# An attention loop with its negation and sums ahead of the copies, and the first weight loads later

## Chip, cores and metric
The kernel runs on one core of a Trainium2 chip. The metric is the device time of one execution in microseconds (us), the median of several runs. The engines work side by side, each through its own instructions in order, and wait for each other by semaphores: TensorE (PE; its weight loads PEld), VectorE (DVE), ScalarE (ACT), GpSimd (POOL), and SyncE (SP), which here only issues DMA transfers.

## What is computed
Attention over a sliding window of 64, then a mixture of experts with one expert a token, then a gated feed-forward layer:

```python
# q, k, v: (4, 8, 576, 64), window 64
scores = np.where(mask, scale * np.matmul(q, k.transpose(0, 1, 3, 2)), -1000000000.0)
attn = np.exp(scores - np.max(scores, axis=-1, keepdims=True))
attn = attn / (np.sum(attn, axis=-1, keepdims=True) + 1e-09)
x = np.matmul(attn, v)                    # as (2304, 512)
# each token goes to one of 8 experts of 288 places: h = relu(x @ w1[e]) @ w2[e]   (512 -> 1024 -> 512)
g = x @ w_gate; val = x @ w_val           # 512 -> 1536
out = (g / (1 + np.exp(-g)) * val) @ w_out
```

## The kernel before
**Stages.** Attention with the logits of the routing fills the first 123 us, the routing itself goes on to about 165 us, and the rest are the experts and the gated layer, which run on PE almost without a gap. The order of every engine's instructions is that in which the Python code emits them.

**Attention.** There are 16 pairs of batch and head pair, each with 9 blocks of 64 queries. Four such blocks make a group, so there are 36 groups (`NG`), and the loop of line 344 has a step `i` for each. Its steps overlap several groups:

- in even steps `scores(i // 2)`: PE writes the masked scores of two groups, `i` and `i + 1`, into two of three banks `ps_s`;
- `maxima(i)` (DVE, L216): the rows' maxima, from `ps_s` to `nm`; `negated(i)` (DVE, L219) multiplies `nm` in place by the negative scale;
- `exponents(i - 1)` (ACT, L226): four activations with `nm` as bias, to `pp`, with the rows' sums in `sm`;
- `transposed(i - 3)`: PE (L241) turns the normalised tile `pn` into a bank `ps_t`, and ACT copies it to `pt` (L249);
- in odd steps `values((i - 5) // 2)` (PE, L256), in even ones `out_x` (DVE, L272) copies its result to `xT` (in the rows `big`); a few steps also have a product for the logits (L280) with its copy (L285);
- `take(i)`: preparation of later queries and keys, mostly one q and one k a step: PE transposes them (L184) into two banks `ps_t`, then DVE (L190), or ACT (L188) for the second half of a k, copies them to `qt` and `kt`. In odd steps it also has POOL copy values, `vw` (L172);
- `norms(i - 1)`: DVE adds a tiny number to the sums (L231) and takes the reciprocal (L232), and POOL multiplies `pp` by it, giving `pn` (L236).

The banks `ps_t` are three in a ring for `pn` transposes and preparations together. `load(h)` issues the DMAs of a head pair's q, k (L163) and v (L167) on SP, three to five pairs ahead. Each waits until its buffer is free, and SP issues in order.

**First weights.** After step 27 (`3 * NC`) the loop emits `convert_move()`, three transfers `raw` (L869) for the gated layer, and `st.load(4)`, four transfers `wraw` (L43) for the experts, 512 KB each. `wraw` is first read in the routing, by ACT (L59, `whi<-wraw`).

Of the kernel before, what the change touches and what calls it, by code (L numbers as in the profile page):

```python
# [68 lines left out]
class Kernel:  # L69
# [30 lines left out]
    def attention(self, ctx):  # L100
        nc = self.nc
        B, H, S, D = self.q.shape
        HP, NC = H // 2, S // 64
# [47 lines left out]
        NG = len(units) // 4  # L151
# [23 lines left out]
        def prep(name, b, hp, x):  # L175

            if name == "v":
                copy_v(b, hp, x)
                return
            if not x:  # L180
                tr[name, b, hp] = kt_p.tile([128, S], F32, name=name + "t")
            ps = ps_t.tile([128, 3, 96], F32, name="ps_t")
            for t in range(3):
                nc.tensor.transpose(ps[:, t, :], raw[name, b, hp][:, 3 * x + t].rearrange("p s d -> p (s d)"),  # L184
                                    self.ident[0:96, 0:96])
            dst = tr[name, b, hp][:, 288 * x:288 * x + 288].rearrange("p (t i) -> p t i", t=3)
            if name == "k" and x:
                nc.scalar.activation(dst, ps, AF.Copy)  # L188
            else:
                nc.vector.tensor_copy(dst, ps)  # L190
# [3 lines left out]
        def scores(G):  # L194

            us = units[8 * G:8 * G + 8]
            for h in range(2):
                SS[2 * G + h] = ps_s.tile([128, 4, 128], F32, name="ps_s")
            for r in range(2):
                first = ([4 - m for m in range(4) if us[2 * m + r][1] == 0] or [0])[0]  # L200
                for h, sl in enumerate(sides):
                    mm(SS[2 * G + h][sides[r]], identb[sl, sl], mask[sl, first:first + 4], start=True, stop=False)
            for m in range(4):
                for r in range(2):
                    b, c, hp = us[2 * m + r]
                    for h, sl in enumerate(sides):
                        k = tr["k", b, hp][sl]
                        kk = k[:, 64 * c - 64:64 * c + 64] if c else k[:, None, 0:64].to_broadcast([64, 2, 64])
                        mm(SS[2 * G + h][sides[r], m, :], tr["q", b, hp][sl, 64 * c:64 * c + 64], kk,
                           start=False, stop=m == 3)  # L210
# [3 lines left out]
        def maxima(g):  # L214
            NM[g] = small.tile([128, 4], F32, name="nm")
            nc.vector.tensor_reduce(NM[g], SS[g], axis=AX.X, op=OP.max)  # L216

        def negated(g):
            nc.vector.tensor_scalar(NM[g], NM[g], -scale, None, op0=OP.mult)  # L219

        def exponents(g):
            ps, nm = SS[g], NM[g]
            PP[g] = work.tile([128, 4, 128], F32, name="pp", bufs=2)
            SM[g] = small.tile([128, 4], F32, name="sm")
            for u in range(4):
                nc.scalar.activation(PP[g][:, u, :], ps[:, u, :], AF.Exp, bias=nm[:, u:u + 1], scale=scale,  # L226
                                     accum_out=SM[g][:, u:u + 1])

        def norms(g, halves=False):
            sm = SM[g]  # L230
            nc.vector.tensor_scalar(sm, sm, 1e-9, None, op0=OP.add)  # L231
            nc.vector.reciprocal(sm, sm)  # L232
            PN[g] = work.tile([128, 4, 128], F32, name="pn", bufs=4)
            for eng, u in ((nc.gpsimd, slice(0, 1)), (nc.vector, slice(1, 4))) if halves else ((nc.gpsimd, slice(0, 4)),):
                n = u.stop - u.start
                eng.tensor_tensor(PN[g][:, u], PP[g][:, u], sm[:, u, None].to_broadcast([128, n, 128]), op=OP.mult)  # L236

        def transposed(g, late=False):
            ps = ps_t.tile([128, 4, 128], F32, name="ps_t")
            for u in range(4):  # L240
                nc.tensor.transpose(ps[:, u, :], PN[g][:, u, :], self.ident)  # L241
            PT[g] = work.tile([128, 4, 128], F32, name="pt", bufs=3)
            if late == 2:
                nc.vector.tensor_copy(PT[g][:, 0:2], ps[:, 0:2])
                nc.scalar.activation(PT[g][:, 2:4], ps[:, 2:4], AF.Copy)
            elif late:
                nc.vector.tensor_copy(PT[g], ps)
            else:
                nc.scalar.activation(PT[g], ps, AF.Copy)  # L249

        def values(G, j0=0, n=8, p=ps_o, name="ps_o"):
            ps = OO[G, j0] = p.tile([128, n, 64], F32, name=name)
            for j in range(j0, j0 + n):
                b, c, hp = units[8 * G + j]
                for h, sl in enumerate(sides):
                    mm(ps[sl, j - j0, :], vw(b, hp)[:, c, h, :], PT[2 * G + h][:, j // 2, sides[j % 2]],  # L256
                       start=True, stop=True)
# [19 lines left out]
        def logits(t0, n, ps_p=ps_o, name="ps_o", act=False):  # L277
            ps = ps_p.tile([128, n], F32, name=name)
            for hp in range(HP):
                mm(ps[32 * hp:32 * hp + 32, :], wgp[:, hp, :], xT[:, hp, t0:t0 + n], start=True, stop=True)  # L280
            LT[t0] = work.tile([128, n], F32, name="lt", bufs=2)
            if act:
                nc.scalar.activation(LT[t0], ps, AF.Copy)
            else:
                nc.vector.tensor_copy(LT[t0], ps)  # L285

        def logits2(t0, n, ps_p=ps_o, name="ps_o"):
            lt = LT[t0]
            k = n // 128
            pl = ps_p.tile([128, k, 128], F32, name=name)  # L290
            for i in range(k):
                nc.tensor.transpose(pl[:, i, :], lt[:, 128 * i:128 * i + 128], self.ident)
            nc.vector.tensor_reduce(self.L[:, t0 // 128:t0 // 128 + k, :],
                                    pl.rearrange("p k (a e) -> p k e a", a=HP)[:, :, 0:NE, :], axis=AX.X, op=OP.add)
# [3 lines left out]
        def load(h):  # L298

            if h < NP:  # L300
                load_rows("q", h // HP, h % HP)
                load_rows("k", h // HP, h % HP)
            if 0 < h <= NP:
                load_v((h - 1) // HP, (h - 1) % HP)
# [13 lines left out]
        for h in reversed(range(NP)):  # L318
            for a in (("k", 1), ("q", 1), ("k", 0), ("q", 0)):

                i = 2 * ((h * NC + 4 * a[1]) // 8) - (1 if h < 2 else 2)
# [10 lines left out]
        for h in range(NR, NP + 1):  # L332

            i = max(ready[h - NR] if h < NP else 0, 2 * (((h - NV) * NC - 1) // 8) + 6 if h > NV else 0)
            loads.setdefault(i + 1, []).append(h)

        def take(i):
            for h, (name, x) in todo.get(i, ()):
                prep(name, h // HP, h % HP, x)
# [4 lines left out]
        for i in range(NG - 1):  # L344
            for h in loads.get(i, ()):
                load(h)
            if i % 2 == 0:
                scores(i // 2)
            maxima(i)
            if i >= 1:  # L350
                exponents(i - 1)
            if i >= 3:
                transposed(i - 3)
            if i % 2 and i >= 5:
                values((i - 5) // 2)
            if late:
                logits2(*late)
                if late[0] + late[1] == 128 * self.n0:
                    window = self.first_window(ps_o.tile([128, 1], F32, name="ps_o"))
                late = None  # L360
            if i % 2 == 0 and i >= 6:
                if done < 1536 and S * (8 * (i - 6) // 2 // (HP * NC)) >= done + 512:
                    late = (done, 512)
                    logits(*late)
                    done += 512
                out_x((i - 6) // 2)
            take(i)
            negated(i)
            if i >= 1:
                norms(i - 1)  # L370
            if i < NC or i % 2:
                next(made, None)
            next(window, None)
            if i == 3 * NC:
                self.convert_move()
                self.st.load(4)

# [772 lines left out]
```

## Time and profile before
| | us |
|---|---|
| median of 3 runs | 837.43 (835.99 to 837.7) |
| profiled execution | 837.32 |
| its span, first to last instruction | 835.5 |

| engine | busy us | share of the span |
|---|---|---|
| PE | 788.7 | 94% |
| PEld | 732.2 | 88% |
| DVE | 514.8 | 62% |
| ACT | 373.9 | 45% |
| POOL | 125.6 | 15% |

A busy share over the whole span mixes the stages. The stage that a change lies in is read by itself, by the busy time in stretches of it and by what ended each wait there. The granted clock of PE stands in tenths of its full 2.4 GHz; 0.5 is its lower level, 1.2 GHz. A busy time of a small instruction includes time in which it was held up after its start.

### The profile page before, as it was taken

How to read it: one execution, taken by the hardware profiler on the slowest of the kernel's cores; microseconds unless marked ns; L12 is line 12 of the kernel's file. 1: busy time of each engine (PE TensorE's matmuls, PEld its weight loads, DVE VectorE, ACT ScalarE, POOL GpSimd, SP SyncE). 2: the span in 40 equal slices, each digit the busy share in tenths (PEclk: the TensorE clock that was granted, in tenths of full speed). 3: DMA queues.
4: the chain of work that ended last, by engine and by line, in shares of the span. 5: the costliest groups of instructions: out<-in, count | busy, mean ns of one | idle time of the engine just before them, and what ended most of it. 6: DMA issues, size and time to landing. Idle time of an engine off the chain costs nothing.

```text
span 835.5 us, 15332 instructions
## 1 busy us (share of the span) xinstructions
PE 788.7 (94%) x5895; PEld 732.2 (88%) x5895; DVE 514.8 (62%) x1078; ACT 373.9 (45%) x947; POOL 125.6 (15%) x206
## 2 busy tenths in 40 slices
PE   7889786499999999999999999999999999999997
PEld 5767665399999999999999999999999999999996
DVE  5787678678888888898774443544453455344322
ACT  3877646346665666575332333323232243222211
POOL 6767643400010000000000000210000011000002
PEclk8999998699999999999999999999999999999999
DMA  9866706669898897777632211331211223220001
GB/s 183 175 149 138 221 2 213 196 200 286 276 288 271 276 287 263 243 258 263 204 118 69 77 51 50 114 114 51 76 52 51 75 89 114 76 68 10 1 1 76
DMA packets 109742, 119.57 MB, mean 143 GB/s; under 512 B 61280, under 2 KB 77664, under 8 KB 109664
## 3 DMA queue, kind: packets, MB, share of 16 engines
q1 hardware_dynamic: 106784, 109.09, 43.2%
q0 software_dynamic: 2880, 9.44, 3.3%
q8 instruction: 49, 0.80, 0.4%
q14 instruction: 29, 0.24, 0.1%
HBM read 99.63 MB, written 18.87 MB: 142 GB/s over the span
## 4 chain that ended last, share of the span: by engine, by line
PE 43%; issue 33%; DVE 2%; POOL 2%; DMA 0%; ACT 0%; POOLq 0%; DVEq 0%; ACTq 0%
PE psw L937 12%; PE psg L937 12%; PE psa L937 11%; PE pso L937 6%; POOL out_dram L1082 1%; PE psw L969 1%; DMA w<-t 0%; DVE wlo L60 0%; PE psw L431 0%; DVE sg L1054 0%; DVE t L890 0%; DVE t L894 0%; ACT xt L929 0%; DVE y L930 0%; POOLq L1146 0%
## 5 line engine op out<-in xcount | busy, mean ns | idle before, releaser
L937 PE MATMUL psg<-y,whi 128*128 128x384 f32 x1152 | 223.1, 336 | 0.0
L937 PEld LDWEIGHTS psg<-y,whi 128*128 128x128 f32 x1152 | 201.6, 188 | 0.0
L60 DVE TENSOR_TENSOR wlo<-wraw,whi 128x512 fp32r<-128x512 f32 x236 | 155.3, 687 | 8.8 <-ACT whi L59 4.3
L59 ACT ACTIVATE whi<-wraw 128x512 fp32r<-128x512 f32 x236 | 136.6, 622 | 2.8 <-ACTq L668 2.8
L1050 DVE TENSOR_TENSOR sg<-sg,psg 128x384 f32<-128x384 f32 x72 | 39.8, 553 | 156.1 <-ACT sg L1049 156.0
L937 PE MATMUL pso<-whi,p 128*128 128x512 f32 x432 | 133.3, 390 | 0.0
L937 PE MATMUL psg<-y,wlo 128*128 128x384 f32 x576 | 123.5, 336 | 0.7 <-DVE sg L1050 0.7
L1049 ACT ACTIVATE sg<-psg 128x384 f32<-128x384 f32 x72 | 35.3, 491 | 174.6 <-PE psg L937 174.6
L937 PEld LDWEIGHTS psg<-y,wlo 128*128 128x128 f32 x576 | 102.5, 188 | 3.8 <-DVE sg L1050 1.2
L937 PEld LDWEIGHTS pso<-whi,p 128*128 128x128 f32 x432 | 80.6, 188 | 14.5
L1056 ACT ACTIVATE p<-sg 128x384 fp32r<-128x384 f32 x72 | 37.8, 525 | 120.7 <-DVE sg L1054 120.7
L1082 POOL DMA_INDIRECT out_dram<-orow,idx x18 | 17.5, 971 | 456.9 <-ACT orow L1080 270.9
L937 PE MATMUL pso<-wlo,p 128*128 128x512 f32 x216 | 84.2, 390 | 0.0
L937 PE MATMUL psw<-xt,whi 128*128 128x288 f32 x512 | 78.5, 296 | 0.0
L937 PE MATMUL psa<-hl,whi 128*128 128x288 f32 x256 | 75.6, 295 | 0.1
L937 PE MATMUL psa<-hh,whi 128*128 128x288 f32 x256 | 75.5, 295 | 0.0
L937 PE MATMUL psa<-hh,wlo 128*128 128x288 f32 x256 | 75.3, 294 | 0.0
L937 PEld LDWEIGHTS psw<-xt,whi 128*128 128x128 f32 x512 | 71.5, 188 | 0.0
L1057 DVE TENSOR_TENSOR p<-sg,p 128x384 fp32r<-128x384 f32 x72 | 40.2, 558 | 42.6 <-ACT p L1056 42.6
L226 ACT ACTIVATE pp<-ps_s,nm 128x128 f32<-128x128 f32 x144 | 51.0, 372 | 25.9 <-DVE sm L231 22.7
L1054 DVE TENSOR_TENSOR sg<-sg,psg 128x384 f32<-128x384 f32 x72 | 39.8, 553 | 21.0 <-PE psg L937 21.0
L926 ACT ACTIVATE hh<-psw 128x288 fp32r<-128x288 f32 x64 | 26.3, 411 | 58.3 <-PE psw L937 58.3
(177 smaller groups left out, 1063.6 us busy)
## 6 DMA issues: line engine op xcount, KB each, us to landing
wraw<-in_moe_w_dram SPq DMA_DIRECT2D x64, 512.0 KB, 5.1
wraw<-w SPq DMA_DIRECT2D x54, 512.0 KB, 3.3
w<-t SPq DMA_DIRECT2D x36, 256.0 KB, 3.6
raw<-in_moe_w_gate_dram SPq DMA_DIRECT2D x12, 512.0 KB, 5.2
raw<-in_moe_w_val_dram SPq DMA_DIRECT2D x12, 512.0 KB, 5.9
raw<-in_moe_w_out_dram SPq DMA_DIRECT2D x12, 512.0 KB, 5.3
rawq<-in_q_dram SPq DMA_DIRECT2D x32, 144.0 KB, 3.4
rawk<-in_k_dram SPq DMA_DIRECT2D x32, 144.0 KB, 3.9
```

The costliest lines, as they stand in the source:

```text
L59: self.nc.scalar.activation(h[sl], t[sl], AF.Copy)
L60: self.nc.vector.tensor_tensor(lo[sl], t[sl], h[sl].bitcast(F32), op=OP.subtract)
L226: nc.scalar.activation(PP[g][:, u, :], ps[:, u, :], AF.Exp, bias=nm[:, u:u + 1], scale=scale, accum_out=SM[g][:, u:u + 1])
L926: nc.scalar.activation(h, x, AF.Relu)
L937: self.nc.tensor.matmul(acc, x, y, start=start and i == 0, stop=stop and i == len(seq) - 1)
L969: nc.tensor.transpose(ps[:, d, :], self.xg[t][r0:r1, 128 * d:128 * d + 128], self.ident[r0:r1, r0:r1])
L1049: nc.scalar.activation(sg, pg, AF.Sigmoid)
L1050: nc.vector.tensor_tensor(sg, sg, pg, op=OP.mult)
L1054: nc.vector.tensor_tensor(sg, sg, pv, op=OP.mult)
L1056: nc.scalar.activation(p[0][:, sl], sg, AF.Copy)
L1057: nc.vector.tensor_tensor(p[1][:, sl], sg, p[0][:, sl].bitcast(F32), op=OP.subtract)
L1082: d = nc.gpsimd.indirect_dma_start(out=self.out, out_offset=bass.IndirectOffsetOnAxis(ap=self.idx[:, 6 * g + t:6 * g + t + 1], axis=0), in ...
```

## The change
`negated(i)` moves from the end of the step to just behind `maxima(i)`. `take(i)` moves behind `norms(i - 1)`. The first weight loads are emitted after step 32 (`NG - 4`, 36 groups) instead of step 27.

```diff
@@ -347,6 +347,7 @@
             if i % 2 == 0:
                 scores(i // 2)
             maxima(i)
+            negated(i)
             if i >= 1:
                 exponents(i - 1)
             if i >= 3:
@@ -364,14 +365,13 @@
                     logits(*late)
                     done += 512
                 out_x((i - 6) // 2)
-            take(i)
-            negated(i)
             if i >= 1:
                 norms(i - 1)
+            take(i)
             if i < NC or i % 2:
                 next(made, None)
             next(window, None)
-            if i == 3 * NC:
+            if i == NG - 4:
                 self.convert_move()
                 self.st.load(4)
```

On DVE, in the middle of the loop, an even step (with `out_x`) and the odd step behind it, before:

```order
L216 TENSOR_REDUCE nm<-ps_s 128x4
L272 COPY big<-ps_o 128x256 x2
L190 COPY qt<-ps_t 128x288
L219 TENSOR_SCALAR nm<-nm 128x4
L231 TENSOR_SCALAR sm<-sm 128x4
L232 RECIPROCAL sm<-sm 128x4
L216 TENSOR_REDUCE nm<-ps_s 128x4
L190 COPY qt<-ps_t 128x288
L190 COPY kt<-ps_t 128x288
L219 TENSOR_SCALAR nm<-nm 128x4
L231 TENSOR_SCALAR sm<-sm 128x4
L232 RECIPROCAL sm<-sm 128x4
```

And after, the same two steps:

```order
L216 TENSOR_REDUCE nm<-ps_s 128x4
L219 TENSOR_SCALAR nm<-nm 128x4
L272 COPY big<-ps_o 128x256 x2
L231 TENSOR_SCALAR sm<-sm 128x4
L232 RECIPROCAL sm<-sm 128x4
L190 COPY qt<-ps_t 128x288
L216 TENSOR_REDUCE nm<-ps_s 128x4
L219 TENSOR_SCALAR nm<-nm 128x4
L231 TENSOR_SCALAR sm<-sm 128x4
L232 RECIPROCAL sm<-sm 128x4
L190 COPY qt<-ps_t 128x288
L190 COPY kt<-ps_t 128x288
```

The negation stands right behind the maxima of its group, the output copies lie between it and the sums, and the copies of q and k end the step.

On POOL, early in the loop (`-` before, `+` after; `below` and `base` are constants of the routing):

```order
 L525 MEMSET below_395 128x18
 L525 MEMSET below_396 128x18
+L236 TENSOR_TENSOR pn<-pp,sm 128x512
 L172 TENSOR_TENSOR vw_141<-vw_141,vone 64x384 x2
 L172 TENSOR_TENSOR vw_141<-vw_141,vone 64x256
-L236 TENSOR_TENSOR pn<-pp,sm 128x512
```

The value copies of an odd step go behind that step's `pn`. All through the loop two `pn` still lie between two groups of value copies, but it is another of the two that follows them.

On SP, at the end of the attention's loads (`rawq`, `rawk`, `vw` are the last two head pairs' rows, `xrows` the row stores after attention):

```order
 L163 DMA rawk<-in_k_dram 96x6x64 x2
 L167 DMA vw_143<-in_v_dram 64x9x64 x2
-L869 DMA raw_1785<-in_moe_w_gate_dram 128x2x512
-L869 DMA raw_1787<-in_moe_w_gate_dram 128x2x512
-L869 DMA raw_1789<-in_moe_w_val_dram 128x2x512
-L43 DMA wraw<-in_moe_w_dram 128x4x256
-L43 DMA wraw<-in_moe_w_dram 128x2x512
-L43 DMA wraw<-in_moe_w_dram 128x4x256
-L43 DMA wraw<-in_moe_w_dram 128x2x512
 L163 DMA rawq<-in_q_dram 96x6x64 x2
 L163 DMA rawk<-in_k_dram 96x6x64 x2
 L167 DMA vw_144<-in_v_dram 64x9x64 x2
```

and directly below these rows:

```order
 L167 DMA vw_140<-in_v_dram 64x9x64 x2
+L869 DMA raw_2056<-in_moe_w_gate_dram 128x2x512
+L869 DMA raw_2058<-in_moe_w_gate_dram 128x2x512
+L869 DMA raw_2060<-in_moe_w_val_dram 128x2x512
+L43 DMA wraw<-in_moe_w_dram 128x4x256
+L43 DMA wraw<-in_moe_w_dram 128x2x512
+L43 DMA wraw<-in_moe_w_dram 128x4x256
+L43 DMA wraw<-in_moe_w_dram 128x2x512
 L425 DMA xrows<-row 128x512 x3
```

The seven weight transfers pass the last head pair's q and k and the last two head pairs' v. On PE and ACT the order of the instructions is that of before.

## Rows read from the trace of the kernel before
**Rows 1.** Busy us by stretch: engines (instructions), PE clock, DMA share, GB/s.
```profile
20.00:80.00 60.00, 53.83 (x970) 43.86 (x963) 45.99 (x136) 45.32 (x202) 43.73 (x52) 0.97 0.73 155
...
101.50:113.00 11.50, 9.99 (x176) 7.29 (x174) 9.30 (x27) 8.12 (x39) 9.42 (x12) 0.99 0.01 2
...
165.00:835.00 670.00, 662.90 (x4004) 633.77 (x4004) 396.17 (x695) 274.21 (x548) 31.70 (x50) 1.00 0.43 140
```
**Rows 2.** PE's waits, 20 to 113 us: us in total, times, longest.
```profile
PE ps_t L241 <- POOL pn L236: 4.7, 8, 0.9
PE ps_t L241 <- ACT pt L249: 3.8, 6, 0.9
...
PE ps_s L202 <- ACT pp L226: 0.7, 2, 0.5
```
**Rows 3.** Timeline, last loads: start, us, what [idle before <- releaser].
```profile
80.02 1.83 SPq L869 DMA_DIRECT2D raw<-in_moe_w_gate_dram  x2
...
84.87 3.18 SPq L163 DMA_DIRECT2D rawq<-in_q_dram  x2
...
88.15 5.13 SPq L163 DMA_DIRECT2D rawk<-in_k_dram  x2
...
93.39 4.14 SPq L167 DMA_DIRECT2D vw<-in_v_dram  x4
...
96.57 0.44 PE L184 MATMUL ps_t<-ident,rawq 96*128 96x96 f32 x3 [2.64 <-DMA rawq<-in_q_dram]
...
98.17 0.68 PE L184 MATMUL ps_t<-ident,rawk 96*128 96x96 f32 x3 [1.16 <-DMA rawk<-in_k_dram]
```
**Rows 4.** Timeline, an odd step in the middle of the loop.
```profile
50.11 0.65 PE L241 MATMUL ps_t<-ident,pn 128*128 128x128 f32 x4 [0.91 <-POOL pn L236]
...
50.28 0.66 DVE L216 TENSOR_REDUCE nm<-ps_s 128x4 f32<-128x512 f32 x1
...
51.65 2.19 POOL L172 TENSOR_TENSOR vw<-vw,vone 64x384 f32<-64x384 f32 x3
...
52.28 0.46 DVE L190 COPY qt<-ps_t 128x288 f32<-128x288 f32 x1 [1.34 <-PE ps_t L184]
...
53.02 0.85 DVE L219 TENSOR_SCALAR nm<-nm 128x4 f32<-128x4 f32 x1
...
53.96 0.37 ACT L226 ACTIVATE pp<-ps_s,nm 128x128 f32<-128x128 f32 x1 [1.79 <-DVE sm L231]
```
**Rows 5.** Busy time in three pairs of groups, columns as in rows 1.
```profile
92.06:101.54 9.48, 5.68 (x83) 4.63 (x82) 5.47 (x18) 4.53 (x21) 3.71 (x5) 0.82 0.75 145
...
101.54:106.02 4.48, 4.06 (x84) 3.38 (x83) 3.92 (x13) 3.52 (x18) 3.51 (x5) 0.99 0.00 0
41.68:46.83 5.15, 4.41 (x84) 3.48 (x84) 4.89 (x14) 4.06 (x20) 3.23 (x5) 1.00 0.71 158
```
**Rows 6.** Timeline, first read of an expert weight.
```profile
125.53 0.64 ACT L59 ACTIVATE whi<-wraw 128x512 fp32r<-128x512 f32 x1
```
**Rows 7.** Timeline, the pair of groups that begins at 41.68 us.
```profile
42.89 0.66 PE L241 MATMUL ps_t<-ident,pn 128*128 128x128 f32 x4
...
43.02 0.69 DVE L216 TENSOR_REDUCE nm<-ps_s 128x4 f32<-128x512 f32 x1
...
43.59 0.60 ACT L249 ACTIVATE pt<-ps_t 128x512 f32<-128x512 f32 x1
43.63 0.74 DVE L272 COPY big<-ps_o 128x192 f32<-128x192 f32 x2
...
44.33 0.63 PE L241 MATMUL ps_t<-ident,pn 128*128 128x128 f32 x4 [0.28 <-POOL pn L236]
```
**Rows 8.** The negations: ns min/median/max, first and last start in us.
```profile
L219 DVE TENSOR_SCALAR nm<-nm x36: 156/158/846, 10.4 to 112.3; 128x4 f32<-128x4 f32 x36
```
**Rows 9.** Groups by line, DVE, 20 to 113 us: count | busy us, mean ns.
```profile
L219 DVE TENSOR_SCALAR nm<-nm 128x4 f32<-128x4 f32 x33 | 10.3, 314 | 0.2
L231 DVE TENSOR_SCALAR sm<-sm 128x4 f32<-128x4 f32 x33 | 9.6, 291 | 1.4 <-ACT pp L226 1.4
```

## Prediction, made before the changed kernel ran
> **What bounds the kernel now.** I read first the busy time by stage. From 165 us to the end TensorE (PE) is busy 662.90 of 670 us [rows 1]: two feed-forward stages in which no other engine matters, and which the change does not touch. It is worth looking only before that. In the attention loop, about 14 to 113 us, PE is busy 53.83 of 60 us between 20 and 80 us [rows 1]. So PE is nearly the bound there too, and no reordering of other engines can give more than PE's idle time.
>
> Second, I asked what ends that idle time. Between 20 and 113 us PE waits 4.7 us (8 times) for POOL's normalised tiles `pn`, 3.8 us (6 times) for ScalarE (ACT) to empty a `ps_t` bank into `pt`, and 0.7 us (twice) for the exponents to give back a scores bank [rows 2]: 9.2 us in 16 places. Apart from these stand two waits for DMA, 2.64 and 1.16 us, one after the other at 96.57 and 98.17 us [rows 3].
>
> Third, the timeline of one pair of groups shows where the 9.2 us start [rows 4]. VectorE (DVE) ends the row maxima at 50.94 (50.28 + 0.66). The negation needs nothing else, but between them stand the copies of a later q and k, which have to wait for PE's transposes: DVE sits idle 1.34 us, copies at 52.28, and negates only at 53.02. ACT, which can't start the exponents without the negated maximum, is idle 1.79 us until 53.96. Exponents, sums, `pn`, and with them ACT's later copy to `pt`, all slide; PE meets the result at its next transpose. Just before, at 50.11, it had waited 0.91 us for `pn` of an earlier group.
>
> Fourth, the DMA waits. SP issues the seven weight transfers (512 KB each, 3.5 MB) from 80.02, then q and k of the last head pair at 84.87 and 88.15 [rows 3]. These two issues take 3.18 and 5.13 us. The queue is full of weights, and PE stands still until q lands.
>
> **The change, part by part.** No instruction is added or removed, and the order on PE and ACT stays the same. Three things move.
>
> *(a) The weight loads.* On SP they now stand behind the last q, k and v. The q issue is then held only by its buffer. The rows do not show when that came free, only that it was no later than 84.87; without the backlog q lands several us before its need at 93.94 (96.57 - 2.64). To price the stall I compare the pair of groups that holds it, 92.06 to 101.54 us, with pairs of the same content (scores, two transposes of `pn`, one q and one k, one value product): 9.48 us against 4.48 (101.54 to 106.02) and 5.15 (41.68 to 46.83) [rows 5]. The gain lies between 9.48 - 5.15 = 4.3 and 9.48 - 4.48 = 5.0 us. That is more than the 3.8 us of waiting, since the granted clock is 0.82 in that stretch and 1.00 or 0.99 in the others: after standing still PE falls to the lower of its two levels, 1.2 instead of 2.4 GHz, for part of the stretch. I take **4.8 us**: 9.48 less the 4.41 us that PE is busy in the pair at 41.68, less the 0.28 us stall of (b).
>
> What does the later load cost? The v loads of the last two head pairs ended their issue at 97.53 (93.39 + 4.14) behind the backlog [rows 3]; without it the weights can follow at that point or before. Even at 97.53, with an issue time of 4.8 us (80.02 to 84.87) and a drain like that of before (first issue at 80.02, q behind it landed by 96.57, so under 17 us for all seven and the q), they are in by about 114 us. They are first read at 125.53 [rows 6], or some 8.7 us earlier after the gains, about 117. The cover is the end of the attention stage, in which next to nothing else is transferred (2 GB/s from 101.5 to 113 us [rows 1]); I cost it at nothing. If it were gone, a late half would hold the first step of the routing by what is missing, at most a few us.
>
> *(b) Negation first.* On DVE the negation of a group follows its maxima at once, and sums and reciprocal come ahead of the copies. In the stretch shown, ACT could start 50.94 + 0.85 (the longest negation) = 51.8 us at the latest, not 53.96. What is late next? Two things. First, the pool `ps_t` has three banks: with two preparations between two `pn` transposes, the second takes the first's bank and waits for ACT's copy. At 42.89 + 0.70 ACT was there on time, copied 0.60 us, and PE still stood 0.28 us at 44.33 [rows 7]. This **floor of 0.28 us** stays in every such pair. Of the 18 pairs three belong to the start, three have a product for the logits between the two transposes, and one holds the DMA stall and is priced in (a): 11 pairs, 3.1 us of the 9.2. Second, the q and k copies are now behind a maximum, a negation, an output copy, and sum and reciprocal. By the rows: maximum done 43.71 [rows 7], negation 0.16 [rows 8], output copies 0.74 [rows 7], sum 0.16 and reciprocal as much again, copy 0.46 [rows 4]: 45.4, that is 3.7 us after the scores began (41.68 [rows 5]), where it was 3.1 (the output copies' end, 44.37, and 0.46). PE wants that bank again after the value product, which in that pair would end about 4.1 us after the scores began without the stall (44.33 - 0.28 + 0.6 for the transpose + 1.1 for the product). Only 0.4 us of slack is left, and it is eaten where a DVE instruction is held up.
>
> That it is held up the trace shows: the negation lasts 156 ns at its shortest and 158 in the median [rows 8], but 314 ns on average, and the sum 291 ns [rows 9], 33 x (156 + 133) ns = 9.5 us above the median in all; the one at 53.02 lasts 0.85 us and ends at 53.87, as POOL's `vw` copies end (51.65 + 2.19 = 53.84) [rows 4]. The Trainium skill has the rule (SBUF — State Buffer, Who interferes with whom): a tensor_scalar that uses both ports and a GpSimd instruction exclude each other, and the second waits for the whole of the first. It speaks against this change, because negation and sums, one run of three small instructions so far, become two separate entries into that queue; by the rule the time would come out at the lock rival's below, 832.5 us.
>
> The new wait of PE for a q bank lies between 0 (no hold-up) and 1.0 us a pair: twice 0.7 us of hold-up (0.85 - 0.16) less 0.4 of slack. I take 0.2, nearer the low end: hold-ups are 0.15 us on average now, and I put them at 0.3 each when the two instructions are apart, 0.6 - 0.4 = 0.2 us a pair, 2.2 us over 11 pairs. So (b) gives 9.2 - 3.1 - 2.2 = **3.9 us**, bounds 9.2 - 3.1 = 6.1 above and 9.2 - 3.1 - 11.0 = -4.9 below.
>
> *(c) POOL.* `pn` of an even group now goes ahead of the odd step's v copies (2.19 us in three), which had delayed it; the `pn` of the next group stands behind them instead, and is wanted half a pair later. Part of the 4.7 us in (b) hangs on this; no price of its own.
>
> The sum: 837.32 us of the profiled execution (span 835.5, the rest outside it; it lies 0.11 below the median of 837.43) less 4.8 less 3.9 = **828.6 us**. Everything behind the attention stage moves forward as a whole.
>
> **The rivals.**
> *The lock takes (b) away.* The small DVE instructions meet POOL so often (POOL is busy 43.73 of 60 us [rows 1]) that the wait for `pn` turns into one for the q bank. For it: the row at 53.02 and the 9.5 us above. Against it: the maxima between are not held up, and DVE still has idle time behind them. Only (a) is left: 837.3 - 4.8 = 832.5, with half of (b) lost or a little more lost than gained 831.5 to 835.
> *Everything goes well.* ACT runs ahead, the new wait stays 0, (b) gives 6.1, and (a) 5.0: 837.3 - 5.0 - 6.1 = 826.2; if the floor goes as well, 823.
> *(a) doesn't do what it says:* q of the last pair is late for another reason, its buffer. Then only (b): 833.4. Against it: no other wait for q or k between 20 and 96 us.
> *Slower.* The q and k copies now wait, behind the sums, for ACT's exponents of the group before. If that and the lock cost PE the whole 1.0 us at the q bank in each of 11 pairs, while the 9.2 us stay, the time is 837.3 - 4.8 + 11 = 843.5. It turns slower than before from 4.8 / 11 = 0.44 us a pair on. Against it: the exponents start earlier by the same change.
>
> **How the numbers follow.** Forecast, 826.5 to 831.5: 0.57. Lock: 0.17. All well: 0.13. Without (a): 0.04. No change to be seen: 0.05; slower: 0.04. A measurement here tells about 0.2%, 1.7 us, from nothing. Faster 0.91, same 0.05, slower 0.04. The range reaches from the better part of the all-well case, 824.5, to the better part of the lock's, 833.5.
>
> **What would show it.** Right: no PE wait for q or k by DMA near 95 us, weights issued behind the last v; ACT's waits for the negation (1.79 us at 53.96) mostly gone; PE's waits for `pn` down to a few tenths, those for `pt` near 0.28 each; the end of attention about 8 us earlier and the rest of the same length. Wrong: PE waits at the q and k transposes for DVE's copies, or DVE busy in nearly all of the loop with negations and sums of 0.5 us and more; or a first weight split that waits for DMA.

## The result, and the profile after

The changed kernel takes 825.95 us in the median (824.54 to 827.45, 4 runs) against 837.10 (835.99 to 837.70, 4 runs): a ratio of 0.986, interval 0.984 to 0.989, 11.2 us faster. The forecast was 828.6, range 824.5 to 833.5. The profiled execution after is the shortest of its four: 824.54 us, span 822.8.

The windows by stretch of the kernel after (columns as in [rows 1]):

```profile
20.00:80.00 60.00, 56.44 (x1052) 46.03 (x1048) 50.41 (x150) 50.49 (x227) 48.62 (x57) 1.00 0.78 169
...
165.00:822.00 657.00, 650.80 (x3915) 622.04 (x3914) 388.61 (x680) 269.57 (x537) 29.55 (x47) 1.00 0.42 138
```

PE is busy 56.44 of 60 us where it was 53.83 [rows 1]; the feed-forward stages are as full as before. What PE waits for between 20 and 100 us, after, which answers to [rows 2]:

```profile
PE ps_t L241 <- ACT pt L249: 5.0, 13, 1.0
PE ps_o L256 <- DVE lt L285: 0.3, 1, 0.3
```

The waits for `pn` are gone from this stretch, and so are those for DMA. What is left is PE's wait for ACT's copy, 11 of the 13 between 0.27 and 0.30 us and two of 0.96. SP's queue around the last loads, after, which answers to [rows 3]:

```profile
74.61 1.84 SPq L163 DMA_DIRECT2D rawq<-in_q_dram  x2
76.54 1.01 SPq L163 DMA_DIRECT2D rawk<-in_k_dram  x2
78.60 6.34 SPq L167 DMA_DIRECT2D vw<-in_v_dram  x4
84.99 1.13 SPq L869 DMA_DIRECT2D raw<-in_moe_w_gate_dram  x2
86.17 0.47 SPq L869 DMA_DIRECT2D raw<-in_moe_w_val_dram  x1
86.68 2.45 SPq L43 DMA_DIRECT2D wraw<-in_moe_w_dram  x4
```

The last q and k issue in 1.84 and 1.01 us at 74.61 and 76.54, where they took 3.18 and 5.13 at 84.87 and 88.15. The seven weight transfers follow at 84.99, and the first split reads one at 111.63 without a wait for DMA:

```profile
111.63 0.64 ACT L59 ACTIVATE whi<-wraw 128x512 fp32r<-128x512 f32 x1
```

Where the time went I read from the starts of PE's scores and the windows between them. The 11 pairs of groups between the scores of group 8 and of group 30, first before, then after; then the pair that held the DMA stall, after (before it is in [rows 5]):

```profile
30.63:92.06 61.43, 54.04 (x983) 43.88 (x982) 47.53 (x145) 47.42 (x212) 45.06 (x53) 1.00 0.71 180
```

```profile
29.11:84.76 55.65, 53.05 (x985) 43.24 (x984) 47.52 (x143) 47.04 (x210) 44.66 (x52) 1.00 0.69 154
...
84.76:89.04 4.28, 4.00 (x83) 3.36 (x82) 3.50 (x13) 4.18 (x19) 3.37 (x4) 1.00 0.85 234
```

The loop's 11 pairs give 61.43 - 55.65 = 5.8 us. In the same two windows PE's waits for other engines fall from 7.4 us in 12 places to 2.5 in 9, all 0.27 to 0.30; the other 0.99 is in PE's busy time, whose ends are modelled. The stalled pair gives 9.48 - 4.28 = 5.2; the pair behind it takes 4.97 instead of 4.48 (one of the waits of 0.96).

Three more differences can't be put down to the change. Up to group 8 it is 1.5 us earlier; the eleven other orders and variants below start group 8 anywhere from 28.1 to 33.3 us. From group 4 to group 8 the clock is 0.84 before and 1.00 after. At 0.99 and 1.00 these two pairs take 10.6 and 10.3 us in e1 and e3 below, and 9.2 to 9.9 in four profiles with the whole new order on DVE (after, after again, e2, e5); so up to about 1 us may be the order's there, which is not shown. The end of attention, from the last scores to the first row transpose, before, after, and in a second profile of the changed kernel:

```profile
106.02:123.26 17.24, 14.24 (x190) 9.70 (x187) 12.03 (x39) 7.65 (x32) 7.59 (x10) 0.90 0.01 2
```

```profile
94.01:109.37 15.36, 12.45 (x191) 8.52 (x187) 12.00 (x39) 7.13 (x30) 8.41 (x10) 1.00 0.22 75
```

```profile
94.12:110.83 16.71, 13.93 (x190) 9.57 (x186) 12.02 (x39) 7.16 (x30) 8.42 (x10) 0.90 0.19 66
```

1.9 us shorter after, but 1.4 of it is missing in the same kernel's other profile: what differs is the granted clock, 0.90 or 1.00, and with it PE's busy time. Nine of the variants below have 1.00 in this stretch and take 15.2 to 15.8 us, in either order. Where it falls in the kernel before, by the windows:

```profile
113.00:115.00 2.00, 0.88 (x13) 0.50 (x12) 1.91 (x8) 1.72 (x9) 1.04 (x1) 1.00 0.00 0
115.00:117.00 2.00, 2.00 (x28) 1.57 (x26) 0.95 (x2) 0.00 (x0) 0.68 (x1) 0.57 0.00 0
```

PE is busy only 0.88 of 2 us, and then the clock is 0.57, close to the lower level, 1.2 GHz. The routing stage behind gives 1.1 us back (42.43 us at 0.76 before, 43.50 at 0.65 after; in six other profiles here 41.7 to 44.9, the longest at the lowest clock). So the profile's 12.7 us are 5.8 + 5.2 - 0.5 = 10.5 from the change and some 2.3 (1.5 + 1.9 - 1.1) from stretches in which the granted clock differs too and the change is not shown to act.

### The profile page after: what moved, and what is told of

The parts are those of the page before. It is cut to its first block, busy times and chain, and to the rows that moved or that the text cites. A ratio compares the mean times of both kernels' runs of the same rounds, so it can differ in the third digit from the quotient of the medians.

```text
span 822.8 us, 15333 instructions
## 1 busy us (share of the span) xinstructions
PE 784.3 (95%) x5895; PEld 729.3 (89%) x5895; DVE 513.3 (62%) x1078; ACT 373.4 (45%) x947; POOL 125.7 (15%) x206
## 4 chain that ended last, share of the span: by engine, by line
PE 44%; issue 34%; DVE 2%; POOL 2%; DMA 1%; ACT 0%; POOLq 0%; DVEq 0%; ACTq 0%
PE psw L937 12%; PE psg L937 12%; PE psa L937 12%; PE pso L937 6%; POOL out_dram L1082 1%; PE psw L969 1%; DMA w<-t 1%; DVE wlo L60 0%; PE psw L431 0%; DVE sg L1054 0%; ACT xt L929 0%; DVE t L890 0%; DVE t L894 0%; DVE y L930 0%; POOLq L1146 0%
```

## The experiments

Two accounts were open. One says that what slows the order of before is the late negation and, with it, the hold-up of small DVE instructions beside POOL. The other says that it is the order in DVE's and POOL's queues: what stands ahead of `pn`. I took the change apart, and for each kernel measured also the **loop**, the time from the scores of group 8 to those of group 30 in its profile, which leaves out the stall and nearly all of the stretches in which the clock varies (the clock is 1.00 in all these loops but e7's, 0.97).

| kernel | loop, us | ratio to before, interval |
|---|---|---|
| before | 61.43 | 1 |
| after; profiled again | 55.65; 55.89 | 0.986 (0.984 to 0.989); 0.986 (0.983 to 0.989) |
| e1 weights only | 61.44 | 0.994 (0.992 to 0.996) |
| e2 loop only | 55.80 | 0.995 (0.993 to 0.997) |
| e3 negation first only | 61.00 | 1.001 (1.000 to 1.002) |
| e4 sums first only | 76.87 | 1.018 (1.016 to 1.020) |
| e5 after, values ahead of `pn` | 58.94 | 0.993 (0.991 to 0.995) |
| e6 after, q and k ahead of the sums | 57.76 | 0.990 (0.988 to 0.993) |
| e7 no negation, sums last | 60.69 | 0.990 (0.989 to 0.992) |
| e8 after without the negation | 55.32 | 0.985 (0.983 to 0.987) |
| e9 after, half the `pt` copy on DVE | 63.77 | 0.998 (0.997 to 1.000) |
| e10 e8 with half the `pt` copy on DVE | 57.75 | 0.991 (0.988 to 0.993) |
| e11 e1 without the value copies | 58.69 | one run, with another result |

**The two parts, each alone.** First the weights, against before:

```diff
-            if i == 3 * NC:
+            if i == NG - 4:
```

> The kernel before, with only the first weight loads moved to step 32. Two-part theory: the loop keeps its 9.2 us of PE waits for pn, pt and scores banks, the DMA wait of 3.8 us and the slow clock behind it go, 4.3 to 5.2 us in all: 837.1 - 4.8 = 832.3 us. Rival (the gain of the weights exists only together with the faster loop, or the loads only collide with something else later): 835.5 us or more, and a DMA wait or a late first weight in the trace.

832.88 us, against 837.61 of before beside it: 4.7 us less (3.1 to 6.4 by the interval), the 4.8 of the forecast, and the loop is that of before to a hundredth. The scores of group 30 and of group 34 start, in e1, at

```profile
90.48 0.41 PE L202 MATMUL ps_s<-mask,identb 64*64 64x512 bf16 x4
...
100.59 0.41 PE L202 MATMUL ps_s<-mask,identb 64*64 64x512 bf16 x4
```

These two pairs take 10.11 us, against 106.02 - 92.06 = 13.96 before and 94.01 - 84.76 = 9.25 after. So the loads alone give 3.9 us there, and the other 0.9 come from the order. Then the loop alone, which is the kernel after with this line turned back:

> The changed order in the loop with the weight loads left at step 27. Two-part theory: what the change gave in all, 11.2 us, less the 4.8 to 5.2 of the weights, so 6 us: 831 us; the DMA wait for the last q stays, between 3 and 6 us, since the loop now arrives earlier at it. Rival (the loop's gain is small and most of the 11.2 us came from the loads): 835 us or more.

832.98 us, 4.6 us less. The loop gains all of its 5.6 us, and the stall grows. PE's waits from 14 to 130 us, the pair that holds the stall, and the start of the scores of group 34, in e2:

```profile
PE ps_t L184 <- DMA rawq<-in_q_dram: 4.6, 1, 4.6
...
PE ps_t L184 <- DMA rawk<-in_k_dram: 2.5, 2, 1.5
```

```profile
84.31:96.16 11.85, 5.71 (x83) 4.66 (x83) 4.75 (x19) 5.40 (x25) 4.11 (x5) 0.80 0.81 179
```

```profile
101.42 0.41 PE L202 MATMUL ps_s<-mask,identb 64*64 64x512 bf16 x4
```

The DMA waits are 7.1 us, more than the 3 to 6 expected, and the time is 2 us above the 831 expected. The pair takes 11.85 us where it took 9.48: PE comes to it earlier, q lands when the backlog lets it. Over the two pairs from group 30 to group 34 the loads are worth (101.42 - 84.31) - 9.25 = 7.9 us in the faster loop and 3.9 in the slow one (e1). The medians alone would hardly tell this: 4.7 + 4.6 = 9.3 against 11.2 together, a difference about as large as the intervals.

**Negation first, alone**, against before:

```diff
             maxima(i)
+            negated(i)
...
             take(i)
-            negated(i)
             if i >= 1:
                 norms(i - 1)
```

> The kernel before with only the negation moved behind the maxima; sums stay behind the q and k copies, loads at step 27. Theory that the late negation started the loop's waits: ACT's waits for it (22.7 us) nearly gone, most of the loop's gain here: 831.5 to 833.5 us. Rival (the sums and POOL's order set the loop's pace): 835.5 to 837.1 us, and PE still waits 3 us or more for pn.

838.62 us: nothing gained, a little above even the rival's range. ACT's waits for DVE's sums and negations fall as meant, from 20.3 us to 5.9 (20 to 100 us). But PE's waits for `pn`, 3.2 us in 5 places there before, rise instead of falling. The waits of PE from 20 to 100 us, DVE's negations there, and part of the timeline, in e3:

```profile
PE ps_t L241 <- POOL pn L236: 9.1, 10, 1.5
```

```profile
L219 DVE TENSOR_SCALAR nm<-nm 128x4 f32<-128x4 f32 x28 | 16.3, 582 | 1.0
```

```profile
44.60 1.04 POOL L236 TENSOR_TENSOR pn<-pp,sm 128x512 f32<-128x512 f32 x1 [0.95 <-DVE sm L232]
...
45.04 0.62 DVE L219 TENSOR_SCALAR nm<-nm 128x4 f32<-128x4 f32 x1
...
45.72 2.19 POOL L172 TENSOR_TENSOR vw<-vw,vone 64x384 f32<-64x384 f32 x3
...
47.98 1.04 POOL L236 TENSOR_TENSOR pn<-pp,sm 128x512 f32<-128x512 f32 x1
...
49.08 0.66 PE L241 MATMUL ps_t<-ident,pn 128*128 128x128 f32 x4 [1.33 <-POOL pn L236]
```

Two things are to be seen. The `pn` that PE waits 1.33 us for runs at 47.98, directly behind three value copies that hold POOL until 45.72 + 2.19 = 47.91. And the negation at 45.04 takes 0.62 us instead of 0.16: the maxima in this order start as soon as the reciprocal frees POOL's `pn`, so the negation falls inside it, and ends at 45.66, as `pn` does (45.64).

**Sums first, alone**, against before:

```diff
-            take(i)
-            negated(i)
             if i >= 1:
                 norms(i - 1)
+            take(i)
+            negated(i)
```

> The kernel before with only the sums and the normalising moved ahead of the q, k and v preparation; the negation stays at the end of the step, loads at step 27. Theory that the late negation started the waits: 836 to 837.5 us, ACT still idle 20 us or more for the negation. Rival (sums and POOL's order set the pace): 831.5 to 833.5 us, PE's wait for pn below 1 us.

852.44 us, 14.8 us slower, which neither account expected. The waits of all engines from 20 to 100 us, in e4:

```profile
ACT pp L226 <- DVE nm L219: 30.6, 22, 3.3
POOL pn L236 <- DVE sm L232: 19.1, 16, 2.6
DVE sm L231 <- ACT pp L226: 15.4, 18, 1.4
```

It is a closed circle: the exponents wait for the negation, which stands behind the sums of the group before, which wait for that group's exponents. PE's loop of 11 pairs grows by 15.4 us. The part that brings most of the gain once the negation is first is, without it, the worst kernel run here.

**Which of the two copies.** From here on three causes stand against each other: *POOL* (the value copies ahead of `pn`), *late sums* (the sums behind the copies of q and k), and *the lock* (small instructions held up). In the kernel after, `take(i)` is split, and one part stands ahead of `norms(i - 1)` again, values in e5, q and k in e6:

```diff
+            take(i, "v")
             if i >= 1:
                 norms(i - 1)
-            take(i)
+            take(i, "qk")
```

> The changed kernel, but POOL's value copies stay ahead of the sums and of pn, as before the change; DVE's order and the loads are the changed ones. Theory POOL (in the run with the negation alone, pn was late because the value copies stood ahead of it): 831 to 833 us and several us of PE waits for pn. Theories lock and late sums: 825.5 to 827.5 us, like the changed kernel.

> The changed kernel, but the copies of q and k stand ahead of the sums again (DVE's order of the run with the negation alone); POOL's value copies stay behind pn, the loads late. Theory POOL: 826 to 828 us. Theory lock (with nothing between the reciprocal and the next maxima, the negation always falls into POOL's pn and is held up, 0.55 us on average) and theory late sums (pn is late because its sums stand behind q and k copies that wait for PE): 832 to 834 us, negation 0.5 us or more on average.

e5: 831.35 us, e6: 829.80, against 838.21 beside them. The loop loses 3.3 us by the values' place and 2.1 by that of q and k. So e5 came as the theory POOL said, but e6 lies between the ranges of the accounts: POOL's order isn't all of it. PE's waits for `pn` from 20 to 100 us in e6:

```profile
PE ps_t L241 <- POOL pn L236: 3.7, 6, 1.0
```

Whether the late sums or the held-up negations (460 ns on average) make e6's 2.1 us this run doesn't separate. In e5 PE's waits from 20 to 100 us and one place of the timeline:

```profile
PE ps_t L241 <- POOL pn L236: 7.0, 9, 1.3
```

```profile
43.09 2.19 POOL L172 TENSOR_TENSOR vw<-vw,vone 64x384 f32<-64x384 f32 x3
...
45.36 1.04 POOL L236 TENSOR_TENSOR pn<-pp,sm 128x512 f32<-128x512 f32 x1
...
46.45 0.65 PE L241 MATMUL ps_t<-ident,pn 128*128 128x128 f32 x4 [1.25 <-POOL pn L236]
```

It is e3's picture again: `pn` starts where the three copies end (45.28). DVE's order in e5 is that of after, so what was moved is POOL's queue alone.

**Is it the hold-up of the small instructions?** A kernel without any negation instruction: the maxima are written negated, and the factor goes into the q copy.

```diff
-            nc.vector.tensor_reduce(NM[g], SS[g], axis=AX.X, op=OP.max)
+            nc.vector.tensor_reduce(NM[g], SS[g], axis=AX.X, op=OP.max, negate=True)
...
+                nc.vector.tensor_scalar(dst, ps, scale, None, op0=OP.mult)
...
-            negated(i)
```

e8 has it in the order of after; e7 has also `take(i)` ahead of `norms(i - 1)`.

> DVE's and POOL's order of the run with the negation alone (preparation ahead of sums), late loads, but without a negation instruction: the maxima are written negated, and the scale goes into the copy of q. Theory lock: the hold-up is gone, 825.5 to 828 us. Theories POOL and late sums: 831 to 834 us with 5 us or more of PE waits for pn, since sums and pn stand where they stood.

> The changed kernel without a negation instruction (negated maxima, scale in the copy of q). All theories: at least as fast as the changed kernel; if the 0.28 us floor at the ps_t bank is all that is left in the loop, 825 to 826 us and no different from it; if held-up negations still cost something, 823 to 825 us.

e8: 826.45 us, as the kernel after; its loop is 0.3 us shorter. e7: 830.03, between the ranges of the accounts, with PE's wait for `pn` back:

```profile
PE ps_t L243 <- POOL pn L238: 7.9, 10, 1.7
```

So with no negation at all, the order of sums and copies makes 60.69 - 55.32 = 5.4 us of the loop. About 1.4 of this is the clock: in e7, behind the wait of 1.70 us for `pn`, it is 0.63 from 49.00 to 53.40 us, and PE is busy 6.04 us in that pair of groups where it is 4.65 in e8. That leaves about 4.0 us; the medians differ by 3.6. The instruction that e8 takes away is worth next to nothing in the order of after. The hold-ups as a whole didn't go with it, though: the sums last 371 ns on average in e8 (200 after).

**The value copies taken away** in e1's order, that is with the negation late as before; they are left out, and the previous block's values stay zero:

```diff
-            nc.gpsimd.memset(vws[i][0:64, 0:1], 0.0)
+            nc.gpsimd.memset(vws[i][0:64], 0.0)
...
             if name == "v":
-                copy_v(b, hp, x)
                 return
```

> The order of before with the late loads (e1), with POOL's value copies left out (so half of each block's values is zero and the result is another; only the attention loop is to be read). Theory POOL (the copies ahead of pn made it late): PE's waits for pn between 20 and 100 us fall from 5.4 to 1 us or less, the loop 3 us or more shorter, though ACT still waits for the negation. Rival (the late negation alone made pn late): 3 us or more of them stay.

PE's and then ACT's waits from 20 to 100 us, in e11:

```profile
PE ps_t L240 <- ACT pt L248: 4.7, 12, 0.6
PE ps_s L201 <- ACT pp L225: 0.9, 3, 0.4
```

```profile
ACT pp L225 <- DVE sm L230: 14.6, 16, 2.6
```

No wait for `pn` is left (e1 has 5.4 us in 7 places), though ACT still waits 14.6 us for late negations (e1: 16.8). The negations last 223 ns here and the sums 165 (e1: 360 and 252), so the value copies are also most of the hold-up; this run doesn't separate the two. The loop is 58.69, 2.75 us shorter than e1's, a little less than the 3 expected. That what is missing to 55.65 is the rest of the order is not shown.

**Can the floor be bought off?** PE's 0.28 us end with ACT's copy of a bank into `pt`. e9 gives half of it to DVE in even steps; e10 does the same to e8.

```diff
-                transposed(i - 3)
+                transposed(i - 3, 0 if i % 2 else 2)
```

> The changed kernel; in even steps the copy from ps_t to pt is shared, two of four blocks on DVE and two on ACT, so that the bank is free about 0.2 us earlier. Theory floor (the 0.28 us in every pair is the bank of ps_t waiting for ACT's copy): the twelve waits of 0.28 us fall to about 0.1 or less, 1.5 to 3 us less than the changed kernel, if DVE's 0.42 us more a pair find room. Rival (DVE is full by now, its copies of q and k come late): as slow as or slower than the changed kernel, with PE waits at q and k transposes for DVE.

> The same with no negation instruction, which gives DVE back what the shared copy takes: theory floor 1.5 to 4 us less than the changed kernel, 822 to 825 us; rival: no better than it.

> The changed kernel again, beside the two that follow: 825 to 827.5 us, the same ratio to the kernel before as at first, 0.984 to 0.989.

Not in this way: 836.37 and 829.37 us, against 826.71 for the kernel after beside them. PE's and ACT's waits from 20 to 100 us in e9, and one place of its timeline:

```profile
PE ps_t L241 <- ACT pt L245: 7.3, 7, 1.2
```

```profile
ACT pt L245 <- DVE pt L244: 19.4, 14, 2.1
```

```profile
44.40 0.56 DVE L219 TENSOR_SCALAR nm<-nm 128x4 f32<-128x4 f32 x1
...
44.87 0.41 DVE L244 COPY pt<-ps_t 128x256 f32<-128x256 f32 x1
...
45.31 0.38 ACT L245 ACTIVATE pt<-ps_t 128x256 f32<-128x256 f32 x1 [1.07 <-DVE pt L244]
...
45.84 0.63 PE L241 MATMUL ps_t<-ident,pn 128*128 128x128 f32 x4 [1.15 <-ACT pt L245]
```

DVE's half stands behind the maxima and a held-up negation, and ACT's half waits for it. The two halves never ran side by side: in all 14 places of e9 from 20 to 100 us, and in the 15 of e10, ACT's starts 0.03 to 0.04 us after DVE's has ended. So the copy takes 0.41 + 0.03 + 0.38 = 0.82 us instead of 0.60, and the bank is free later, not earlier. Both halves write one tile `pt` and read one bank; which of the two keeps them apart no run tells, and whether two halves at the same time would lower the floor stays untested. What e10 does show is the floor from the other side. PE's waits there from 20 to 100 us:

```profile
PE ps_t L243 <- ACT pt L247: 5.9, 11, 0.6
```

The usual wait is 0.56 us instead of 0.28 (e8): it grew by about what the copy did. No kernel here is faster than the one after by more than the intervals.

## Why the forecast held, step by step

**(a), the weights: right.** 4.8 us forecast; 4.7 alone by the medians (e1), 3.9 alone by e1's trace, and 5.2 for the stalled pair in the trace after, where the order sped up the pair too. The 0.4 us above the forecast are in PE's busy time: the 4.41 us of the pair at 41.68 count 0.40 us of the next scores, begun at 45.97, and after it is 4.00. Loading later shows no wait for DMA after, as said; e1 has one of 0.7 us for `wraw`. What the step missed is that its worth depends on the loop: 7.9 us by e2.

**(b), the loop: the sum too small, its working wrong.** Forecast 3.9 us, bounds 6.1 and -4.9; measured 5.8 - 0.5 = 5.3 in the forecast's own split. Against e1, which has the loads alone, the order gives more: 5.8 + 0.9 = 6.7 us by the traces and 11.2 - 4.7 = 6.5 by the medians, above the upper bound. That bound counted PE's waits only, but PE's busy time fell too, by 0.99 us in the loop. Its four steps:

- *The floor of 0.28 us* stands as worked out: 0.27 to 0.30 us in 11 places from 20 to 100 us, the 3.1 us of the forecast. The row in [rows 7] didn't yet show it, since it names `pn`, which in that place ended at 44.21, within 0.02 us of ACT's copy (43.59 + 0.60 = 44.19):

```profile
43.17 1.04 POOL L236 TENSOR_TENSOR pn<-pp,sm 128x512 f32<-128x512 f32 x1 [0.41 <-DVE sm L232]
```

  After, `pn` ends well before the copy (below), and e10 lengthens the wait with the copy.
- *The new wait for a q bank*, put at 2.2 us, is the term that was mis-sized. PE has no such wait after; PE's weight loads have one of 0.25 us (below). In its place came two waits of 0.96 us for `pt`.
- *Hold-ups of 0.3 us each*: they did not rise as a whole. Negation and sum, from 20 to 100 us, after:

```profile
L219 DVE TENSOR_SCALAR nm<-nm 128x4 f32<-128x4 f32 x32 | 10.4, 323 | 1.1
...
L231 DVE TENSOR_SCALAR sm<-sm 128x4 f32<-128x4 f32 x31 | 6.2, 200 | 0.5 <-ACT pp L226 0.5
```

  The negation 323 ns, as before [rows 9], the sum 200 instead of 291 (346 and 249 in the second profile after). Where the order does raise them is e3 (582): there nothing lies on DVE between the reciprocal that frees `pn` and the next maxima, and with the copies of q and k out of that gap the mean rises from 323 to 460 in e6 too. The Trainium skill's rule (SBUF — State Buffer, Who interferes with whom), that a tensor_scalar which uses both ports and a GpSimd instruction exclude each other, agrees with e3's rows, where the negation ends at 45.66 and `pn` at 45.64. The lock rival's time, 832.5 us, did not come: PE did not wait for a q bank, and with no negation at all the loop is only 0.3 us shorter (e8). What the sums' hold-ups cost is not shown.
- *The late negation as the start of the 9.2 us: wrong.* It explained ACT's idle time, and that went (19.9 us to 2.9, waits for L231 from 20 to 100 us); it did not explain PE's. Negation first alone gains 0.4 us in the loop (e3). With it in place, the norms ahead of the copies gain the other 5.4 (e3 to after; e7 to e8, without a negation, says about 4.0 without the clock). Yet the norms alone lose 15.4 (e4). Negation first is what makes the other move possible, not what earns the time.

**(c), POOL: the mechanism was named, but "no price of its own" was wrong.** It is 3.3 of the loop's 5.8 us (e5), and 4.3 to 4.9 us by the medians (831.35 - 838.21 = -6.9, against -11.2 and -11.8 of the kernel after). A stretch of the timeline after shows how the place works:

```profile
44.17 1.04 POOL L236 TENSOR_TENSOR pn<-pp,sm 128x512 f32<-128x512 f32 x1 [0.77 <-DVE sm L232]
...
45.18 0.60 ACT L249 ACTIVATE pt<-ps_t 128x512 f32<-128x512 f32 x1
...
45.28 2.19 POOL L172 TENSOR_TENSOR vw<-vw,vone 64x384 f32<-64x384 f32 x3
...
45.93 0.63 PE L241 MATMUL ps_t<-ident,pn 128*128 128x128 f32 x4 [0.30 <-ACT pt L249]
...
47.88 1.04 POOL L236 TENSOR_TENSOR pn<-pp,sm 128x512 f32<-128x512 f32 x1 [0.41 <-ACT pp L226]
...
48.11 0.28 PEld L184 LDWEIGHTS ps_t<-ident,rawk 96*128 96x128 f32 x3 [0.25 <-DVE qt L190]
```

`pn` is done at 45.21, PE needs it at 45.63 and waits only for ACT's copy; the 2.19 us of values come behind it, and the next `pn` isn't wanted for half a pair. In e5 the same two stand the other way round, and PE waits 1.25 us.

**The total.** 828.6 against 825.95. In the profile the change gave 10.5 us where 8.7 were forecast: 0.4 + 1.4 on (a) and (b). That it came so near is in part luck, since (b) put the gain down to the late negation, which alone earns nothing; the sum came from counting PE's waits, whatever their cause. The rest of the difference between the two profiles lies outside the loop, mostly where the clock differs, which the forecast had no term for and which goes either way; so attention ends 13.9 us earlier (123.26 to 109.37), not about 8.

**The rivals.** *Everything well* (826.2) came closest, and its conditions came true: ACT runs ahead, the new wait stayed 0, the floor of 3.1 us stayed. Its 6.1 us too were put down to the late negation. *The lock* fell, and so did *(a) doesn't do what it says* (e1). *Slower* has its mechanism in e4: a queue that closes on itself through ACT's exponents. I had seen it at the copies of q and k; it sits at the negation, and negation first is what opens it.

**Open.** How much of the values' 3.3 us is their place on POOL and how much the hold-ups that they put on DVE; e5 and e11 change both. What makes the 2.1 us of q and k (e6). Whether a copy shared at the same time would lower the floor. Why the granted clock in the end of attention and in the routing differs between two executions of one kernel.

## What to carry to other kernels

A wait names the instruction that came late; look next at what stands ahead of that instruction in its own queue, since a bulk copy there can cost more than the late input that the waits show on another engine. Try the parts of a reordering one by one and in pairs: here one part alone is worth nothing, another alone costs 15 us, and together they gain 5.8 in the loop. Put large prefetches behind the last small loads that share their queue, and expect their price to grow as the code ahead of them gets faster.

## What the runs showed of the hardware

The 0.28 us floor is the same to 0.02 us in 11 places of one profile and comes back in the second one; it was worked out from the three banks and the 0.60 us copy. No run here changed the banks; with a copy of 0.82 us it is 0.56 (e10). Two copies from one bank to one tile, given to DVE and ACT, ran one after the other in all 29 places (e9, e10). A negation of 128x4 elements, 0.156 us at its shortest [rows 8], averaged 0.67 us in e4 and 0.58 in e3, and 0.22 where POOL's value copies were gone (e11). And the same kernel's end of attention took 15.36 and 16.71 us in two executions, with the granted clock 1.00 and 0.90: a difference of 1 to 2 us between two profiles there says nothing of a change in the loop.
